# VectorE held to program order from block 2 on, with attention cut into finer steps, in a fused attention and Strassen MLP kernel

## The chip, the cores and the metric

The kernel runs on one core of a Trainium2 chip. A core has five engines that are used here: TensorE (PE, matmuls; its weight loads are shown apart as PEld), VectorE (DVE), ScalarE (ACT), GpSimd (POOL) and SyncE (SP, which here only issues transfers). They run side by side, each through a queue of its own, and wait for each other by semaphores. The metric is the time of one execution on the device, in microseconds (us), as a median of several runs. The profile is of one such execution; its span runs from the first to the last instruction and is a little shorter than the time.

## The reference, cut to what matters

```python
# q, k, v: (8, 8, 576, 64) f32, batch B, heads H, sequence S, head size D
kv  = einsum('bhsd,bhse->bhde', k, v)
out = einsum('bhsd,bhde->bhse', q, kv)
rms = sqrt(mean(out * out, axis=-1) + 1e-6)
att = out / rms * g_norm
x = att.transpose(0, 2, 1, 3).reshape(4608, 512)      # B*S tokens, H*D features
h = x @ w_in                                          # 512 -> 2048, w_in comes as float64
g = maximum(0.01 * h, h)
result = g @ w_out                                    # 2048 -> 512, w_out comes as float64
```

Attention has no softmax: a 64 x 64 matrix `kv` for each head, a product with `q`, and a division by a root mean square. Then come two dense layers with a leaky ReLU between them. The 4608 tokens are worked on in nine blocks of 512 (block 0 to block 8). A batch has 576 tokens, so a block boundary cuts through each batch: the tokens of batch b fill the end of block b and the beginning of block b + 1.

## The kernel before: the parts that matter here

Block 0 is a plain matrix product, because the weights are still arriving and being rounded to f32 (ScalarE and VectorE do that). From block 1 on both dense layers are Strassen products in Winograd's form: seven products of half-sized matrices in place of eight, with sums before and after them. From block 2 on the first layer (`h`) is cut so twice, 49 small products. The sums that belong to the weights are formed once; the sums over `x`, over `g` and over the results are formed by VectorE and GpSimd in every block, while TensorE goes on.

A block from 2 on has four parts (`c` = 0 to 3) of seven steps (`t` = 0 to 6). Call `7 * c + t` the slot, 0 to 27. In each slot TensorE does one step of `h` for this part, one step of the second layer (`o`), which runs some slots later for the part before, and in some slots a piece of attention for a later block.

```python
pin = tc.keep_in_program_order     # a pinned instruction keeps its place among the pinned of its engine;
                                   # the others are placed by the scheduler of the language's tile layer
ps_att = tile_pool(bufs=2, PSUM)   # two banks, tag "att": kv_ps and o_ps of attention share them
ps_m   = tile_pool(bufs=1, PSUM)   # six banks: ha, hb, hc, hd for h, oa, oc for o

def matmul(*args, **kw):
    pin(nc.tensor.matmul(*args, **kw))              # L112: all of TensorE's matmuls

def copy_kv(b, kv_ps):
    for i in range(2):
        nc.vector.tensor_copy(kvs[b % 2][:, i::2, :], kv_ps[i])      # L315

def add(eng, out_, a, b_, minus=False, pinned=False):
    ins = eng.tensor_tensor(out_, a, b_, ...)                        # L557: nearly all sums
    if pinned: pin(ins)

def outputs(b, lo, hi, e, sums):                    # one half (e) of q @ kv for some columns
    o_ps = [ps_att.tile([P, n], tag="att") for _ in range(2)]
    o_products(b, lo, hi, e, o_ps)                  # 8 matmuls that read kvs[b % 2] and qT
    for l in range(2):
        ...                                         # ACT square (L343); for e == 1 DVE adds it (L347)
    for l in range(2):
        nc.scalar.activation(x[:, 2 * l + e, :], o_ps[l], func=AF.Copy, scale=...)   # L349

def divide(lo, hi, sums):
    for l in range(2):
        nc.vector.transpose(t, sums[l])             # L356
        nc.vector.tensor_reduce(rms[:, l, :], ...)  # L357
    nc.scalar.activation(rms, rms, func=AF.Sqrt, ...)                # L359
    nc.vector.reciprocal(rms, rms)                  # L360
    for l in range(2):
        nc.scalar.copy(t, ...)                      # L363 "spread"
        nc.vector.transpose(inv, t)                 # L366
        nc.vector.tensor_mul(to, to, inv)           # L368

def tail_of(b, lo, hi):                             # three steps: e = 0, e = 1, divide
    ...

def attention(b, apart=True):                       # a generator; each yield ends a step
    # steps 1 to 3: turn q of pair 0 | turn q of pair 1, kv products of both | ask for loads
    # steps 4 to 7: turn q of pair 2 | turn q of pair 3 | kv products of both | copy_kv, ask for loads
    # then the tail for block b (512 - 64 b tokens), and the tail for block b + 1 (64 (b + 1) tokens)

ORDER = (1, 2, 6, 5, 7, 3, 4)                       # step t of h and of o does product ORDER[t]
# o: products 1, 6, 7, 4 go to bank oa and 2, 5, 3 to bank oc. After each product the bank is added
# to o by DVE, or, in part 0 where it is the first for its quarter of o, copied by ACT.
# So steps go oa, oc, oa, oc, oa, oc, oa, and the next part begins with oa again.

def product_h_two(i, c, quarters, to):
    into = {1: (0, True), 2: (0, False), 6: (1, True), 5: (3, True), 7: (3, False), 3: (1, False), 4: (2, True)}
    for t, k in enumerate(ORDER):
        ...                                         # 4 matmuls to ha or hc, 3 to hb or hd (128x128)
        # fresh: ACT copies both banks; else (products 2, 7, 3: t = 1, 4, 5) DVE adds both
        yield
    add(nc.vector, g21, ...); add(nc.vector, g11, ...)                   # seven sums on DVE
    add(nc.vector, g22, ...); add(nc.vector, g12, ...); add(nc.vector, g22, ...)
    add(nc.vector, g21, ...); add(nc.vector, g21, ...)
    for t in (g11, g12, g22, g21): relu(t)          # ACT, L729
    sums_of(c, to)                                  # four sums on POOL: s1, s2, s3, s4

A_SLOTS = (1, 3, 5, 8, 10, 11, 13, 14, 15, 17, 18, 19, 21)      # one step of attention in each

for i in range(1, NB):
    for c in range(NC):
        for t in range(7):
            go(h_steps, 1)
            go_o()                                  # one step of o (its step 0 falls in slots 2, 9, 16, 23)
            ...                                     # block 1: weight sums
            if 7 * c + t in A_SLOTS: go(a_steps, 1)
            load_some()
            # last part: t = 2: go(a_steps), sums over the x of the next block; t = 3, 4: inner sums on POOL
        go(h_steps)                                 # the seven g sums and what follows
```

In block 1 the first layer is a Strassen product of one level (`product_h`), which used banks `ha` and `hc` in all four parts. In block 0 attention's steps are put in by a table of half-steps: `12, 13, 15, 16, 18, 20, 22, 23, 24, 25, 26, 27`; the last three are the tail of 128 columns for block 2.

Of the kernel before, what the change touches and what calls it, by code (L numbers as in the profile page):

```python
# [23 lines left out]
def kernel(  # L24
# [63 lines left out]
    ps_m = ctx.enter_context(tc.tile_pool(name="ps_m", bufs=1, space=bass.MemoryType.PSUM))  # L88

    pin = tc.keep_in_program_order  # L90


    NW = U * NE * P
# [218 lines left out]

    def copy_kv(b, kv_ps):
        for i in range(2):
            nc.vector.tensor_copy(kvs[b % 2][:, i::2, :], kv_ps[i])  # L315

    def kv_tiles():
        return [ps_att.tile([P, NP // 2, D], F32, tag="att", name="kv_ps") for _ in range(2)]
# [1 line left out]
    def t2k(n, name):  # L320
        home = {"tag": name, "bufs": 1} if name[:3] == "sum" else {"tag": "t2k", "bufs": 3}
        return work.tile([P, n], F32, name=name, **home)

    def x_of(lo, hi):
        return block(lo // NT)[:, :, lo % NT:lo % NT + hi - lo]
# [9 lines left out]
    def outputs(b, lo, hi, e, sums):  # L335


        x, n = x_of(lo, hi), hi - lo
        o_ps = [ps_att.tile([P, n], F32, tag="att", name="o_ps") for _ in range(2)]
        o_products(b, lo, hi, e, o_ps)  # L340
        for l in range(2):
            sq = t2k(n, "sq" if e else f"sum{l}")
            nc.scalar.activation(sq, o_ps[l], func=AF.Square)  # L343
            if e == 0:
                sums.append(sq)
            else:
                nc.vector.tensor_add(sums[l], sums[l], sq)  # L347
        for l in range(2):
            nc.scalar.activation(x[:, 2 * l + e, :], o_ps[l], func=AF.Copy, scale=g_sb[:, e:e + 1])  # L349

    def divide(lo, hi, sums):
        x, n = x_of(lo, hi), hi - lo
        rms = work.tile([P, 2, n // E], F32, tag="rms", name="rms", bufs=2)
        for l in range(2):
            t = t2k(n, "turned")
            nc.vector.transpose(t, sums[l])  # L356
            nc.vector.tensor_reduce(rms[:, l, :], t.rearrange("p (a i) -> p a i", i=E),  # L357
                                    axis=AX.X, op=ALU.add)
        nc.scalar.activation(rms, rms, func=AF.Sqrt, scale=1.0 / D, bias=eps_sb)  # L359
        nc.vector.reciprocal(rms, rms)  # L360
        for l in range(2):
            t = t2k(n, "spread")
            nc.scalar.copy(t.rearrange("p (a i) -> p a i", i=E),  # L363
                           rms[:, l, :].unsqueeze(2).to_broadcast([P, n // E, E]))
            inv = t2k(n, "inv")
            nc.vector.transpose(inv, t)  # L366
            to = x[:, 2 * l:2 * l + 2, :]
            nc.vector.tensor_mul(to, to, inv.unsqueeze(1).to_broadcast([P, 2, n]))  # L368

    def tail_of(b, lo, hi):  # L370
        sums = []
        for e in range(2):
            outputs(b, lo, hi, e, sums)
            yield
        divide(lo, hi, sums)
        yield

    def attention(b, apart=True):

        qT = qTs[b] = work.tile([P, NP, S], F32, tag="qT", name="qT")  # L380
        kv_ps = kv_tiles()

        def turn(p):
            q_in = q_ins.pop((b, p))
            nc.vector.transpose(
                qT[:, p, :].rearrange("p (t s) -> p s t", s=T),
                q_in.rearrange("p (s d) -> p s d", d=D)[:, :, :32])

        for m in range(2):
            turn(2 * m)  # L390
            yield
            turn(2 * m + 1)
            if m:
                yield
            attention_kv(b, m, kv_ps)
            pairs_next = [(b + m, p) for p in ((2, 3) if m == 0 else (0, 1)) if b + m < B]
            if apart or m == 0:
                for nxt in pairs_next[:1 if apart else 2]:
                    if apart:
                        to_load.extend((*nxt, what) for what in ("q", "kv"))  # L400
                    else:
                        load_pair(*nxt)
            yield
            if apart:
                if m:
                    copy_kv(b, kv_ps)
                for nxt in pairs_next[1:]:
                    to_load.extend((*nxt, what) for what in ("q", "kv"))
                yield
        if not apart:  # L410
            copy_kv(b, kv_ps)
            yield
        for i in (b, b + 1):
            yield from tail_of(b, max(i * NT, b * S), min((i + 1) * NT, (b + 1) * S))

    def first_attention():

# [137 lines left out]

    def add(eng, out_, a, b_, minus=False, pinned=False):
        ins = eng.tensor_tensor(out_, a, b_, op=ALU.subtract if minus else ALU.add)  # L557
        if pinned:
            pin(ins)

    def sides_w1(c):
# [104 lines left out]
    def sides_x(i):  # L666
# [10 lines left out]
        sides = {1: b11, 2: b21, 3: b22, 4: t4, 5: t1, 6: t2, 7: t3}  # L677

        def sums():
            add(nc.vector, t1, b12, b11, True)  # L680
            add(nc.vector, t2, b22, t1, True)
            add(nc.vector, t3, b22, b12, True)
            add(nc.vector, t4, b21, t2, True)

        batches, quarters, at = [], {k: {} for k in ORDER}, 0
        upper, lower = (x[:, h:h + 2, :].rearrange("p r (t v n) -> p t r v n", t=2, v=2)
# [19 lines left out]
                else:  # L706
                    add(nc.gpsimd, t4, y21, t2, True)

        return sides, quarters, sums, inner

    def strassen(which, left, right, done):


        banks = {}
        for i in ORDER:
            b = "a" if i in (1, 6, 7, 4) else "c"
            if i in FRESH:
                banks[b] = ps_m.tile([P, 2, N2], F32, tag=f"{which}{b}", name=f"{which}_{b}")
            bank = banks[b]
            for part in range(2):  # L720
                for r in range(2):
                    matmul(bank[:, part, :], lhsT=left(i, part, r), rhs=right(i, part, r),
                           start=i in FRESH and part == 0 and r == 0, stop=(r == 1),
                           skip_group_check=True)
            done(i, bank.rearrange("p u (v n) -> p (u v) n", v=2))
            yield
# [20 lines left out]
    def product_h(c, w_sides, x_sides, to):  # L747

        g11, g21, g22, g12 = g_of(c)

        def done(i, bank):

            if i == 1:
                nc.scalar.copy(g11, bank)
            elif i == 5:
                nc.scalar.copy(g22, bank)
            elif i == 2:
                add(nc.vector, g11, bank, g11, pinned=True)
                relu(g11)
            elif i == 6:  # L760
                nc.scalar.copy(g21, bank)
            elif i == 3:
                add(nc.vector, g21, bank, g21, pinned=True)
                relu(g21)
            elif i == 7:
                add(nc.vector, g22, bank, g22, pinned=True)
                relu(g22)
            else:
                relu(g12, bank)

        yield from strassen("h", lambda i, part, r: w_sides[i][:, part, r, :],
                            lambda i, part, r: x_sides[i][:, r, :], done)
        sums_of(c, to)

    def product_h_two(i, c, quarters, to):
# [22 lines left out]
        g11, g21, g22, g12 = g_of(c)  # L798
        add(nc.vector, g21, qa[:, :, 0, :], qa[:, :, 1, :])
        add(nc.vector, g11, qa[:, :, 0, :], qc[:, :, 0, :])  # L800
        add(nc.vector, g22, g21, qa[:, :, 2, :])
        add(nc.vector, g12, g22, qa[:, :, 3, :])
        add(nc.vector, g22, g22, qc[:, :, 1, :])
# [6 lines left out]
    def product_o(n, g_sides, os, finish):  # L810
# [10 lines left out]
        def done(i, bank):  # L821
# [11 lines left out]
            elif i == 4:  # L833
                sums(1)

        yield from strassen("o", lambda i, part, r: g_sides[i][:, 2 * r + part, :],
                            lambda i, part, r: w_sides[i][:, r, :], done)

    def go(steps, n=None):
# [13 lines left out]
    def first_block(between):  # L853
# [26 lines left out]
        for t in range(4):  # L880
# [3 lines left out]
            else:  # L884
# [3 lines left out]
    first_attention()  # L888
    steps = {i: tail for tail in [tail_of(0, NT, S)] for i in (6, 8, 10)}
    steps.update((i, a1) for a1 in [attention(1, False)]  # L890
                 for i in (12, 13, 15, 16, 18, 20, 22, 23, 24, 25, 26, 27))
    loaded, rounded = 7, 5

    def between(n, half):
# [14 lines left out]

    first_block(between)  # L910
    x_sides, _, sums, _ = sides_x(1)
    sums()
    h_sides, more = sides_w1(0)
    more()
    for part in range(2):
# [2 lines left out]
        combine(0, part)  # L918

    A_SLOTS = (1, 3, 5, 8, 10, 11, 13, 14, 15, 17, 18, 19, 21)  # L920

    LAG = 2
    o_queue, waited = collections.deque(), 0
# [5 lines left out]
            o_queue.popleft()  # L929

    for i in range(1, NB):
        a_steps = attention(i + 1) if i + 1 < B else iter(())
        os = {}
        one = i == 1
        for c in range(NC):
            g_sides = {}
            h_steps = product_h(c, h_sides, x_sides, g_sides) if one else \
                product_h_two(i, c, quarters, g_sides)
            for t in range(7):
                go(h_steps, 1)  # L940
                if waited == LAG:
                    go_o()
                elif o_queue:
                    waited += 1
                if one:
# [6 lines left out]
                    if t == 5 and c < NC - 1:  # L952
                        more_h()
                        combine(c + 1, 1)
                if 7 * c + t in A_SLOTS:
                    go(a_steps, 1)
                load_some()
                if c == NC - 1 and i + 1 < NB:
                    if t == 2 + one:
                        go(a_steps)  # L960
                        x_sides, new_quarters, sums, inner = sides_x(i + 1)
                        sums()
                    elif t == 3 + one:
                        inner(0)
                    elif t == 4 + one:
                        inner(1)
            go(h_steps)
            if c == NC - 1 and i + 1 < NB:
# [37 lines left out]
```

## Time and profile before

| what | value |
|---|---|
| time, median of 3 runs (range) | 940.5 us (938.89 to 941.13) |
| span of the profiled execution | 937.3 us, in a run of 939.01 us |
| mean granted TensorE clock | 0.998 |
| blocks 0 and 1, up to the first two-level product | 236.5 us |
| block 2, 3, 4, 5, 6, from its first `h` product to that of the next block | 100.38, 99.30, 98.30, 98.69, 98.67 us |
| block 7 (no attention left) | 92.17 us |
| DMA, mean over the span | 213 GB/s |

The page of the profile gives busy times of the engines, the chain of work that ended last, and groups of equal instructions by line and tile. A view of the waits says which engine sat idle before which instruction, and what ended that idle time. The timeline lists single instructions or runs of equal ones: start in us, length in us, engine, line, operation, tiles, count, and in square brackets the idle time ahead of it. A matmul of f32 is recorded as two instructions, so that four matmuls of the program show as x8.

### The profile page before, as it was taken

Reading aid. Unit: us, or ns where it says so; the run is one execution under the profiler, and the core shown is the slowest. Engines: PE = TensorE matmul, PEld = TensorE weight load, DVE = VectorE, ACT = ScalarE, POOL = GpSimd, SP = SyncE. Lnnn points to the kernel's source line nnn. Section 1 sums busy time; section 2 is a strip of 40 time slices with the busy share of each in tenths; the row PEclk is TensorE's granted clock in tenths of the full one; section 3 lists DMA queues with packets and bytes.
Section 4 is the critical chain, followed back from the end, with each engine's and each line's share of the span. In section 5 each row is a group of like instructions: output and inputs, shape, how many; then the busy total and the mean of one; then the engine's idle time right before and its main releaser. Section 6 shows DMA issues by size and latency. Waiting matters only on the chain.

```text
span 937.3 us, 17990 instructions
## 1 busy us (share of the span) xinstructions
PE 921.7 (98%) x7076; PEld 774.7 (83%) x7076; DVE 597.8 (64%) x992; ACT 328.2 (35%) x659; POOL 319.1 (34%) x318
## 2 busy tenths in 40 slices
PE   8999999999999999999999999999999999999997
PEld 6544436878998899889988999899988999999996
DVE  3866894578357755596648854785578755554554
ACT  3543632242134422442234323432344233223321
POOL 2000353977622352216210722262225522532222
PEclk9999999999999999999999999999999999999999
DMA  8999925985499569956896688757856675667632
GB/s 258 189 227 244 268 100 166 292 296 164 157 321 275 163 189 274 309 160 177 255 300 205 188 238 294 225 171 236 257 171 182 195 216 183 184 196 219 188 114 90
DMA packets 90067, 200.05 MB, mean 213 GB/s; under 512 B 9856, under 2 KB 42112, under 8 KB 89984
## 3 DMA queue, kind: packets, MB, share of 16 engines
q1 hardware_dynamic: 79392, 186.85, 68.5%
q10 hardware_dynamic: 10144, 10.88, 3.5%
q8 instruction: 56, 0.92, 0.4%
q0 software_dynamic: 448, 1.18, 0.3%
q14 instruction: 27, 0.22, 0.1%
HBM read 172.39 MB, written 26.48 MB: 212 GB/s over the span
## 4 chain that ended last, share of the span: by engine, by line
PE 83%; DVE 7%; DMA 6%; ACT 2%; issue 1%; SPq 0%; ACTq 0%; DVEq 0%
PE o_a L112 22%; PE o_c L112 17%; PE h_ha L112 10%; PE h_hc L112 8%; PE h_hb L112 7%; PE h_hd L112 6%; PE h_a L112 3%; PE o_acc L112 3%; PE h_c L112 2%; PE h_ps L112 2%; DVE g L557 2%; PE o_ps L112 2%; PE kv_ps L112 2%; DMA pairs<-in_k_dram 1%; DMA q_in<-in_q_dram 1%
## 5 line engine op out<-in xcount | busy, mean ns | idle before, releaser
L557 POOL TENSOR_TENSOR gs<-g 128x512 f32<-128x512 f32 x64 | 80.4, 1277 | 446.8 <-ACT g L729 446.8
L557 DVE TENSOR_TENSOR o<-o_c,o 128x512 f32<-128x512 f32 x88 | 60.6, 689 | 98.7 <-PE o_c L112 97.0
L112 PE MATMUL o_a<-pairs,gs 128*128 128x256 f32 x512 | 121.1, 379 | 0.0
L557 DVE TENSOR_TENSOR o<-o_a,o 128x512 f32<-128x512 f32 x104 | 71.2, 685 | 78.0 <-PE o_a L112 78.0
L793 ACT COPY w_all<-h_ha 128x512 f32<-128x512 f32 x84 | 48.9, 582 | 198.6 <-PE h_ha L112 196.7
L729 ACT ACTIVATE g<-g 128x512 f32<-128x512 f32 x124 | 77.4, 630 | 102.3 <-DVE g L557 99.6
L112 PEld LDWEIGHTS o_a<-pairs,gs 128*128 128x128 f32 x512 | 93.0, 190 | 10.3
L112 PE MATMUL o_a<-w,g 128*128 128x256 f32 x256 | 61.1, 381 | 3.9 <-DVE o L557 3.6
L112 PEld LDWEIGHTS h_ha<-stage,w_all 128*128 128x128 f32 x448 | 58.0, 191 | 7.0 <-issue 2.4
L112 PE MATMUL o_c<-w,g 128*128 128x256 f32 x256 | 60.5, 379 | 0.0
L112 PE MATMUL o_c<-w,gs 128*128 128x256 f32 x256 | 60.5, 379 | 0.0
L112 PE MATMUL o_c<-pairs,gs 128*128 128x256 f32 x256 | 60.5, 379 | 0.0
L112 PE MATMUL o_a<-pairs,g 128*128 128x256 f32 x256 | 60.5, 379 | 0.0
L112 PE MATMUL h_ha<-stage,w_all 128*128 128x128 f32 x448 | 60.1, 277 | 0.0
L112 PE MATMUL h_ps<-xT,w_all 128*128 128x512 f32 (+1 forms) x136 | 58.0, 571 | 0.2 <-DVE w_all L249 0.2
L112 PE MATMUL o_acc<-w,g 128*128 128x512 f32 x128 | 58.0, 597 | 0.0
L112 PEld LDWEIGHTS o_a<-w,g 128*128 128x128 f32 x256 | 46.4, 190 | 10.1 <-DVE o L557 3.5
L557 POOL TENSOR_TENSOR pairs<-w_all 128x512 f32<-128x512 f32 x8 | 10.5, 1318 | 127.9 <-DMA stage<-in_moe_w_in_dram 97.2
L557 DVE TENSOR_TENSOR w_all<-h_hc,w_all 128x512 f32<-128x512 f32 x56 | 38.6, 689 | 22.7 <-PE h_hc L112 18.5
L557 DVE TENSOR_TENSOR g<-g,pairs 128x512 f32<-128x512 f32 x84 | 52.9, 684 | 0.0
L112 PEld LDWEIGHTS o_c<-w,gs 128*128 128x128 f32 x256 | 46.5, 190 | 5.2
L112 PEld LDWEIGHTS o_c<-pairs,gs 128*128 128x128 f32 x256 | 46.5, 190 | 5.2
(168 smaller groups left out, 1956.0 us busy)
## 6 DMA issues: line engine op xcount, KB each, us to landing
w_all<-w SPq DMA_DIRECT2D x196, 448.0 KB, 4.1
pairs<-w SPq DMA_DIRECT2D x56, 512.0 KB, 4.5
out_dram<-o ACTq DMA_DIRECT2D x36, 256.0 KB, 4.5
v_in<-in_v_dram SPq DMA_DIRECT2D x29, 288.0 KB, 5.6
k_in<-in_k_dram SPq DMA_DIRECT2D x28, 288.0 KB, 5.6
q_in<-in_q_dram SPq DMA_DIRECT2D x56, 144.0 KB, 6.5
q_in<-in_q_dram SPq DMA_DIRECT2D x56, 140.0 KB, 6.3
w<-stage SPq DMA_DIRECT2D x12, 512.0 KB, 4.6
```

The source lines that it names most:

```text
L112: pin(nc.tensor.matmul(*args, **kw))
L557: ins = eng.tensor_tensor(out_, a, b_, op=ALU.subtract if minus else ALU.add)
L729: nc.scalar.activation(t, t if src is None else src, func=AF.Prelu, alpha=SLOPE)
L793: nc.scalar.copy(q[:, at], banks[tag])
```

## The change

From block 2 on every VectorE instruction is pinned, so that VectorE does its work in the order in which the program is written, and no longer in the order that the scheduler picks. So that the written order is a good one, attention is cut finer (the division into five steps in place of one), its steps get slots of their own, and they are put between the slot's `h` step and its `o` step. The last two of a batch's steps fall into slots 3 and 4 of the next block. The sums over `x` are spread over slots 22 to 24. The first two of the seven `g` sums are made ahead of the `o` step of slot 6 of a part, the other five after it. In block 1, `h` takes banks `ha`, `hc` and `hb`, `hd` by turns. In block 0 the last three steps of attention move from half-steps 25, 26, 27 to 26, 28, 29. The arithmetic is the same.

The purpose is that a sum which TensorE is waiting for (an `o` bank that has to be added before it can be written again) doesn't stand behind a long piece of attention in VectorE's queue.

```diff
+    def in_turn(ins):
+        if steady:
+            pin(ins)
...  # copy_kv, the transposes, reductions, reciprocals and products of attention: in_turn(...)
     def divide(lo, hi, sums):
...
+            if l:
+                nc.scalar.activation(rms, rms, func=AF.Sqrt, scale=1.0 / D, bias=eps_sb)
+            yield                                   # step: transpose and reduce, one l each
+        in_turn(nc.vector.reciprocal(rms, rms))
...      # ACT: both spreads
+        yield
+        for l in range(2):
+            in_turn(nc.vector.transpose(inv, spread[l]))
+            in_turn(nc.vector.tensor_mul(to, to, ...))
+            yield
...  # attention(b, fine=True): the two tails, seven steps each, are taken in this order
+        for tail in (0, 0, 0, 0, 0, 1, 0, 0, 1, 1, 1, 1, 1, 1):
+            next(tails[tail])
+            yield
...
     def add(eng, out_, a, b_, minus=False, pinned=False):
-        if pinned:
+        if pinned or steady and eng is nc.vector:
             pin(ins)
...  # product_h
-        yield from strassen("h", ...)
+        yield from strassen((("ha", "hc"), ("hb", "hd"))[c % 2], ...)
...  # product_h_two
         add(nc.vector, g11, qa[:, :, 0, :], qc[:, :, 0, :])
+        yield
         add(nc.vector, g22, g21, qa[:, :, 2, :])
...
-                 for i in (12, 13, 15, 16, 18, 20, 22, 23, 24, 25, 26, 27))
+                 for i in (12, 13, 15, 16, 18, 20, 22, 23, 24, 26, 28, 29))
...
+    FINE_SLOTS = {1: 1, 2: 1, 4: 1, 9: 1, 10: 2, 11: 2, 12: 1, 15: 1, 16: 1, 17: 2, 18: 1, 19: 2,
+                  22: 1, 24: 1, 25: 1}
+    LATE_SLOTS = (3, 4)
...
+        one = i == 1
+        steady = not one
+        late, a_steps = a_steps, attention(i + 1, fine=not one) if i + 1 < B else iter(())
...
             for t in range(7):
+                slot = 7 * c + t
                 go(h_steps, 1)
+                if not one:
+                    if t == 6:
+                        go(h_steps, 1)              # two of the g sums
+                    if slot in LATE_SLOTS:
+                        go(late, 1)
+                    for _ in range(FINE_SLOTS.get(slot, 0)):
+                        go(a_steps, 1)
+                    if i + 1 < NB:
+                        if slot == 22:
+                            x_sides, new_quarters, sums, inner = sides_x(i + 1)
+                        if slot in (22, 23, 24):
+                            go(sums, 2 if slot == 23 else 1)
+                        if slot == 24:
+                            inner(0)
+                        elif slot == 25:
+                            inner(1)
+                    load_some()
                 ...                                 # then the o step, as before
```

## The prediction

> **What bounds the kernel now.** I read the page's busy times and its chain first.
>
> ```profile
> PE 921.7 (98%) x7076; PEld 774.7 (83%) x7076; DVE 597.8 (64%) x992; ACT 328.2 (35%) x659; POOL 319.1 (34%) x318
> PE 83%; DVE 7%; DMA 6%; ACT 2%; issue 1%; SPq 0%; ACTq 0%; DVEq 0%
> ```
>
> TensorE is busy for 98% of the span and carries 83% of the chain. Since no matmul is removed, the change can only win the time in which TensorE stands still. The waits of TensorE by what ended them (line, who was waited for, total us, times, longest):
>
> ```profile
> PE o_a L112 <- DVE o L557: 3.6, 3, 1.8
> PE o_ps L112 <- ACT xT L349: 1.3, 1, 1.3
> PE h_a L112 <- ACT g L729: 0.7, 1, 0.7
> ```
>
> These three are what the change aims at. The other waits fall in the first 31 us or after the last matmul. To see where the 3.6 us are I read the timeline around the end of block 2 (start, length):
>
> ```profile
> 319.23 0.83 PE L112 MATMUL h_hb<-stage,w_all 128*128 128x128 f32 x6
> 319.74 1.14 DVE L368 TENSOR_TENSOR xT<-xT,inv 128x512 f32<-128x512 f32 x1
> 320.80 0.43 DVE L366 STREAM_TRANSPOSE inv<-spread 128x256 f32<-128x256 f32 x1
> 321.16 0.65 DVE L557 TENSOR_TENSOR o<-o_a,o 128x512 f32<-128x512 f32 x1
> 321.86 1.99 PE L112 MATMUL o_a<-w,g 128*128 128x256 f32 x8 [1.80 <-DVE o L557]
> ```
>
> This is slot 23. Bank oa's last product must be added before the next part's first product may overwrite it, and the add stands behind attention's division. The same place costs 0.73 us at 421.17 in block 3. In blocks 4 to 6 I compared the start of the o_a matmul with that of the h_hb matmul ahead of it: 0.67 us in quiet slots, but 618.15 - 617.21 = 0.94 in block 5 and 716.83 - 715.89 = 0.94 in block 6. The third wait of 1.11 us is at 920.83, in the last part of the last block.
>
> A quiet slot gives the unit for everything below (block 8, slot 25):
>
> ```profile
> 906.24 0.38 PE L112 MATMUL h_ha<-xT,w_all 128*128 128x128 f32 x2
> 907.40 0.69 DVE L557 TENSOR_TENSOR w_all<-h_ha,w_all 128x512 f32<-128x512 f32 x1 [0.27 <-PE h_ha L112]
> 907.80 1.89 PE L112 MATMUL o_a<-pairs,gs 128*128 128x256 f32 x8
> 908.07 0.56 DVE L557 TENSOR_TENSOR pairs<-h_hb,pairs 128x384 f32<-128x384 f32 x1
> 106.43 0.46 DVE L315 COPY kv<-kv_ps 128x128 f32<-128x128 f32 x2
> ```
>
> (The last line, from block 0, is the pair of copies that the reckoning of slot 11 needs.) With T the slot's start: h takes TensorE until T+1.56, o until T+3.29, where the next slot begins. VectorE adds the first h bank from T+1.16 to T+1.85 and the second to T+2.39; the add of an o bank can start 1.93 after its matmuls began (907.80 to 909.73).
>
> **What the Trainium skill says.** "PSUM — Partial Sum Buffer", section "Engine vs sequencer instructions", says that VectorE's queue is strictly first in, first out and that matmuls start and complete in program order. The trace agrees: at 321.86 TensorE stands for an add that waits for nothing but its turn. So the order of the two queues decides, and one can read it off the built programs without any time. "SBUF — State Buffer", section "Who interferes with whom", says that a VectorE instruction with two SBUF inputs and a GpSimd instruction that reads SBUF exclude each other, and the second waits for the first to end. The trace agrees: GpSimd's sum of g at 619.71 began 0.07 us behind a VectorE product of 1.07 us and took 2.14 us, where its like take 1.28. "Perfetto Trace Analysis", section "Identifying the Most-Contended Engine", warns that busy matmul time overstates; weight loads are the better measure. In the stretch from 335.2 to 434.4 us (most of block 3) they are 88.83 of 99.2 us, and since the distances between o products are 3.29 us throughout, I take TensorE as really full.
>
> **The change part by part.**
>
> Block 0: the wait of 1.29 us at 126.40 is attention's second o_ps product of 128 columns, one half-step after the first, when ScalarE has not yet emptied the banks. Now it comes two half-steps later, each about 3.5 us of matmuls. All of it should go: -1.3.
>
> Block 1: the wait of 0.69 us at 162.18 is the second part's first product, for bank ha that ScalarE is still reading. With two pairs of banks it goes: -0.7.
>
> Blocks 2 to 6, slot 23: 1.80 + 0.73 + 0.27 + 0.27 + 0.05 (block 7, start of o_a at 739.96) = 3.1 us. In the new order only small pieces stand ahead of that add. -3.1, less what comes back in slot 22 below.
>
> New wait, slot 11. FINE_SLOTS gives slot 11 two steps: step 7, which is copy_kv, and step 8, attention's first o_ps products. Those matmuls read kvs and take the two banks that kv_ps held, so they need the copies twice over. In the built order TensorE's queue has for slot 11: h_ha, h_hb, o_ps, o_a. VectorE's has: add of h_ha, add of h_hb, two copies, and both copies are now pinned behind the adds. By the quiet slot, which is the same step of h (product 7): adds end at T+2.39, the second copy starts about 0.06 before that and two take 0.46 (the pair at 106.43), so they end at T+2.79; with 0.1 for the semaphore (the add at 321.16 ended at 321.81 and TensorE began at 321.86; at 920.83 it was 0.15) o_ps starts at T+2.89. It could have started at T+1.65 (0.09 after h, as o_ps at 303.69 after o_a). That is 1.24 us in which TensorE stands, and nothing later gives it back, because TensorE is full. Five blocks have it (batches 3 to 7, in blocks 2 to 6): 5 x 1.24 = +6.2. Before, the copies ran some ten us ahead of the products: the first at 278.8, the o_ps at 288.7.
>
> Slot 22. New ahead of the critical add: transpose and reduce of one l (for 256 to 512 columns 0.41 + 0.40 up to 0.69 + 0.68), and one x sum (0.65). I count from S, the start of slot 20 in which the part ends, with offsets from the last part of block 8 (S = 912.82) and 0.6 from one queued VectorE sum to the next. The first g sum starts at S+1.8 (914.59), the second ends by S+3.0; the oa add starts at S+3.5 (914.38 + 1.93); five g sums end at S+7.1; the oc add of slot 21 ends at S+7.7; the h adds of slot 22 (which starts at S+6.58) end at S+8.9. Then come 0.7 to 1.3 of transpose and reduce, then 0.6, so the add starts at S+10.2 to S+10.8 and frees the bank at S+11.0 to S+11.6. TensorE wants it at S+11.43 (two slots and h of 1.56 further on, from S+3.29 each). That is nearly free. But GpSimd makes its four sums of the part at about S+8 to S+13, and the x sum has two SBUF inputs, so it may wait up to one of those sums (1.28). With half of that, the five blocks lose about 0.1, 0.3, 0.4, 0.6 and 0.7 = 2.1; without it 0.1. I take +1.2.
>
> Slot 1 of each block: one q transpose (1.24) ends at S+10.15, before the add is ready at S+10.07 + 0.04, so it costs nothing.
>
> The tail. At the end of block 8 the add of o22 from oa now stands after two g sums and not after three. It can't start before 916.40, while VectorE is free at 915.8. The five remaining sums, then two o adds follow, all 0.6 later; the last bank is free at 921.3 and not at 920.7: +0.6.
>
> Sum: -1.3 - 0.7 - 3.1 + 6.2 + 1.2 + 0.6 = +2.9, so 940.5 + 2.9 = 943.4 us.
>
> **Rivals.**
>
> First: slot 11 costs nothing, for instance since the adds of h come earlier than in my quiet slot or the copies slip ahead. Then it is 943.4 - 6.2 = 937.2 us. For it speaks that the slots look as if they had been chosen with care; against it the two orders, which leave no room.
>
> Second: in strict order VectorE meets many small waits, which the scheduler had filled with other work. VectorE is at 64%, so no single queue is too long, but a q transpose that waits for its transfer (6.5 us from issue to landing, and 4.6 us of such waits before) would hold every add behind it. Against it: the q loads are asked for seven slots, some 23 us, ahead of the slot that turns them. If each of five blocks lost another 2 us, it would be 953.
>
> Third: GpSimd's lock bites in slot 22 in full, or also in slots 3 and 4 (products of 1.1 to 1.8 us). That adds 2 to 3 us: 946.
>
> **Range and chances.** The gains are bounded by the trace at 5.1 us, so the time can't fall under 935.4, which is 0.5% less. The losses rest on one wait, counted five times, that I hold for nine parts in ten sure, with 0.3 us either way, and on two smaller ones. Runs of the kernel before differ by 2.2 us. So 938.5 to 947 us 8 times in 10. Faster by over 2% (under 921.7) is ruled out by the waits there are: 0.01, kept for what I don't see. Slower by over 2% (above 959.3) needs the second rival at twice its size: 0.02. Within 2%: 0.97.
>
> **What would show it.** In TensorE's waits the three lines above shrink: o_ps on ACT xT and h_a on ACT g are gone, o_a on DVE o keeps about 1.7 us at the tail and up to 1 us in each slot 23. A new line stands on top: o_ps waiting for DVE kv (copy_kv), five times about 1.2 us. Blocks 2 to 6, from one first h product to the next, take 99.6 to 100.3 us each in place of 98.3 to 100.4, block 4 (98.3, without a wait now) showing the loss most plainly. I am wrong if that line is missing, or if TensorE waits at other places for more than 2 us in all.

## The result, and the profile after

| | before | after |
|---|---|---|
| time, median (range) | 940.8 us (938.89 to 942.32, 4 runs) | 945.8 us (943.97 to 947.01, 4 runs) |
| ratio after / before | | 1.0052, 95% interval 1.0027 to 1.0078 |
| span of the profiled execution | 937.3 us | 944.6 us |
| start to the first `h` product of block 0 | 28.60 us | 30.20 us |
| block 0, from there to the first `h` product of block 1 | 119.24 us | 118.54 us |
| block 1 | 88.64 us | 87.89 us |
| blocks 2 to 6 | 100.38, 99.30, 98.30, 98.69, 98.67 us | 100.31, 100.31, 100.32, 100.31, 100.32 us |
| block 7 | 92.17 us | 92.12 us |
| block 8 and the end | 113.31 us | 114.28 us |

The kernel became 0.5% slower. The spans differ by 7.3 us. 1.6 of that lies ahead of all work that was changed: the first products wait for the input's transfers, and over all profiles of this study, of whatever kernel, that point lies between 28.5 and 30.4 us. Where the change acts, the profiles differ by -0.70 (block 0), -0.75 (block 1), +6.2 (blocks 2 to 6) and +0.97 (the end): +5.7 us.

The page of the kernel after shows the busy times and the chain that ended last:

```profile
PE 923.4 (98%) x7076; PEld 780.9 (83%) x7076; DVE 611.1 (65%) x992; ACT 327.9 (35%) x659; POOL 320.9 (34%) x318
PE 88%; DVE 6%; DMA 3%; issue 1%; POOL 1%; ACT 1%; DVEq 0%; ACTq 0%; POOLq 0%
```

The busy shares say nothing of the loss: all are as before. Of the chain TensorE has 88% in place of 83%, and yet the time is longer. The waits of TensorE (who, for whom, total us, times, longest) do say it:

```profile
PE o_ps L118 <- DVE kv L321: 5.5, 6, 1.0
PE o_a L118 <- DVE o L582: 4.5, 6, 2.1
PE o_acc L118 <- ACT g L896: 0.7, 1, 0.7
```

The two waits for ScalarE that the change aimed at are gone (`o_ps` on `xT`, `h_a` on `g`), but all three lines here hold losses of the new order. The first has five new waits of 1.0 in slot 11 of blocks 2 to 6 (the sixth, 0.5, was there before, in the first attention). The second was 3.6 in three waits, long ones in blocks 2 and 3, and is 4.5 in six: a wait in slot 23 of each block and one of 2.1 at the end, where it was 1.1. The third is new.

The timeline of slot 11 of block 2 after the change:

```profile
276.78 0.69 DVE L582 TENSOR_TENSOR w_all<-h_ha,w_all 128x512 f32<-128x512 f32 x1 [0.20 <-PE h_ha L118]
277.45 0.56 DVE L582 TENSOR_TENSOR pairs<-h_hb,pairs 128x384 f32<-128x384 f32 x1
277.93 0.48 DVE L321 COPY kv<-kv_ps 128x128 f32<-128x128 f32 x2
278.36 0.97 PE L118 MATMUL o_ps<-qT,kv 64*32 64x320 f32 x16 [1.01 <-DVE kv L321]
```

The copies of `kv` stand behind both adds of `h`, and TensorE stands until they are done: taken singly, one product starts at 278.36, 0.15 after the end of the first copy (278.21), and the others from 278.56 on, 0.15 after the end of the second (278.41). This slot takes 5.25 us in block 4; with the copies made earlier it takes 3.97 (below).

The end of part 2 of the same block, slots 22 and 23:

```profile
318.24 2.50 POOL L582 TENSOR_TENSOR gs<-g 128x512 f32<-128x512 f32 x2 [19.51 <-ACT g L753]
319.08 0.43 DVE L363 STREAM_TRANSPOSE turned<-sum 128x256 f32<-128x256 f32 x1
319.55 0.42 DVE L364 TENSOR_REDUCE rms<-turned 128x8 f32<-128x256 f32 x1
319.89 1.40 DVE L582 TENSOR_TENSOR w_all<-xT 128x512 f32<-128x512 f32 x1
321.21 0.68 DVE L582 TENSOR_TENSOR o<-o_a,o 128x512 f32<-128x512 f32 x1
321.94 1.99 PE L118 MATMUL o_a<-w,g 128*128 128x256 f32 x8 [0.48 <-DVE o L582]
```

The sum over `x` takes 1.40 us, and ends 0.55 after GpSimd's pair of sums (318.24 + 2.50 = 320.74). The add that TensorE waits for stands behind it. In block 6 the transpose and the reduction are twice as large, so that the `x` sum comes later in the queue, and still it ends 0.55 after GpSimd's pair:

```profile
719.51 2.50 POOL L582 TENSOR_TENSOR gs<-g 128x512 f32<-128x512 f32 x2 [20.39 <-ACT g L753]
721.69 0.87 DVE L582 TENSOR_TENSOR w_all<-xT 128x512 f32<-128x512 f32 x1
722.48 0.68 DVE L582 TENSOR_TENSOR o<-o_a,o 128x512 f32<-128x512 f32 x1
```

That is why slot 23 takes 4.03 to 4.04 us in all five blocks, 0.75 more than the 3.29 of a quiet slot, whatever the length of the pieces ahead. The waits of before, uneven (100.38 in block 2, 98.30 in block 4), became the same loss of 1.28 + 0.75 in each.

The last part of block 8, first before and then after:

```profile
916.40 0.68 DVE L557 TENSOR_TENSOR o<-o_a,o 128x512 f32<-128x512 f32 x1
917.00 0.68 DVE L557 TENSOR_TENSOR g<-g,w_all 128x512 f32<-128x512 f32 x1
917.60 1.89 DVE L557 TENSOR_TENSOR g<-g,pairs 128x512 f32<-128x512 f32 x3
920.83 1.96 PE L112 MATMUL o_a<-w,g 128*128 128x256 f32 x8 [1.11 <-DVE o L557]
```

```profile
922.64 0.69 DVE L582 TENSOR_TENSOR o<-o_a,o 128x512 f32<-128x512 f32 x1 [0.43 <-PE o_a L118]
923.25 1.48 DVE L582 TENSOR_TENSOR g<-g,w_all 128x512 f32<-128x512 f32 x2
924.76 2.02 DVE L582 TENSOR_TENSOR g<-g,pairs 128x512 f32<-128x512 f32 x3
926.70 0.69 DVE L582 TENSOR_TENSOR o<-o_c,o 128x512 f32<-128x512 f32 x1
928.13 1.96 PE L118 MATMUL o_a<-w,g 128*128 128x256 f32 x8 [2.07 <-DVE o L582]
```

Two things add up to the 0.96 more. VectorE stands for 0.43 ahead of the `oa` add, where before it made a third `g` sum. And the five sums after it take 926.70 - 923.25 = 3.45 us, 0.69 each, where the four before took 2.40 (917.00 to 919.40), 0.60 each. In the written order, which is pinned now, three of them read or overwrite what the sum just ahead of them touched; the scheduler had set such pairs apart. Taken singly, these three start 0.72 to 0.79 after the sum ahead of them, and the other two, like the `oc` add, about 0.61 after it.

### The profile page after: what moved, and what is told of

It reads as the page before. It is cut to its first block, busy times and chain, and to the rows that moved or that the text cites. A ratio compares the mean times of both kernels' runs of the same rounds, so it can differ in the third digit from the quotient of the medians.

```text
span 944.6 us, 17997 instructions
## 1 busy us (share of the span) xinstructions
PE 923.4 (98%) x7076; PEld 780.9 (83%) x7076; DVE 611.1 (65%) x992; ACT 327.9 (35%) x659; POOL 320.9 (34%) x318
## 4 chain that ended last, share of the span: by engine, by line
PE 88%; DVE 6%; DMA 3%; issue 1%; POOL 1%; ACT 1%; DVEq 0%; ACTq 0%; POOLq 0%
PE o_a L118 22%; PE o_c L118 18%; PE h_ha L118 10%; PE h_hc L118 8%; PE h_hb L118 7%; PE h_hd L118 6%; PE o_acc L118 4%; PE h_ps L118 4%; PE o_ps L118 2%; PE kv_ps L118 2%; PE h_a L118 1%; PE h_c L118 1%; DMA pairs<-in_v_dram 1%; PE h_b L118 1%; DVE w_all L582 1%
## 5 line engine op out<-in xcount | busy, mean ns | idle before, releaser
L582 DVE TENSOR_TENSOR g<-g,pairs 128x512 f32<-128x512 f32 x84 | 55.6, 689 | 1.9
L118 PEld LDWEIGHTS o_c<-w,g 128*128 128x128 f32 x256 | 46.4, 190 | 8.6 <-issue 3.1
```

## The experiments

The theory after the comparison: the loss of blocks 2 to 6 is two places, both of them pieces that program order now holds in front of (or behind) an add that frees a bank. The copies of `kv` cost 1.28 a block; the first `x` sum costs 0.75, by GpSimd's exclusion more than by its length. The rival: strict order costs many small waits, and moving a piece only shifts them.

**The copies of `kv` left to the scheduler.** Only the two copies are not pinned; in the built order they then come right behind the q transpose of slot 10.

```diff
-            in_turn(nc.vector.tensor_copy(kvs[b % 2][:, i::2, :], kv_ps[i]))
+            nc.vector.tensor_copy(kvs[b % 2][:, i::2, :], kv_ps[i])
```

> The changed kernel with one thing undone: the two copies of kv are not pinned. The built VectorE queue then has them right behind the q transpose of slot 10, ahead of the o add and of slot 11's h adds; TensorE's queue and the loads stay. Theory (the copies stand behind the h adds of slot 11): the five waits of o_ps on DVE kv go, each slot 11 shrinks from 5.25 us (block 4) to 3.97 as slot 12, so -1.28 x 5 = -6.4 us against the changed kernel, about 939.4 us, 0.998 to 1.000 of the kernel before. Rival (the two steps in one slot are too close whatever the queue's order, since o_ps needs the banks of kv_ps): the waits stay and the time stays at about 945.8.

Measured: 940.7 us, ratio to before 1.0006 (0.9995 to 1.0017). In block 2 the copies are done long before the products that need them:

```profile
274.72 0.49 DVE L321 COPY kv<-kv_ps 128x128 f32<-128x128 f32 x2 [3.14 <-PE kv_ps L118]
278.08 0.77 PE L118 MATMUL o_ps<-qT,kv 64*32 64x320 f32 x16
```

Slot 11 takes 4.18, 4.08, 3.97, 3.86 and 3.76 us in blocks 2 to 6 (attention's products get smaller), where it took 5.46, 5.36, 5.25, 5.13 and 5.04: 1.28 in each. Blocks 2 to 6 take 99.03 to 99.05. Slot 23 stays at 4.03 to 4.05. So by the profiles the pinned copies are worth 6.4 us, more than the whole loss. The medians are 5.1 apart (945.8 and 940.7), within their scatter.

**The first `x` sum one slot later.**

```diff
-                        if slot == 22:
+                        if slot == 23:
                             x_sides, new_quarters, sums, inner = sides_x(i + 1)
-                        if slot in (22, 23, 24):
-                            go(sums, 2 if slot == 23 else 1)
+                        if slot in (23, 24):
+                            go(sums, 3 if slot == 23 else 1)
```

> The changed kernel with the first sum over x moved from slot 22 to slot 23, so that only the transpose and the reduce of attention stand ahead of the add that frees bank oa. Theory (the x sum holds the add up): the five waits of o_a on DVE o in slot 23 go (0.75 us each with the refill), -3.75 us against the changed kernel: about 942.0 us, ratio 1.001. Rival (transpose and reduce are what is too long): the waits shrink by half at most in the blocks with few columns (256) and stay in those with many (448, 512): about 944.5 us.

Measured: 943.25 us, ratio to before 1.0030 (1.0021 to 1.0038). Slot 23 takes 3.28 to 3.29 in all blocks, blocks 2 to 6 take 99.56 to 99.58, and slot 11 is as in the changed kernel. Slots 22 and 23 of block 2 in this kernel's timeline:

```profile
318.43 2.50 POOL L582 TENSOR_TENSOR gs<-g 128x512 f32<-128x512 f32 x2 [19.53 <-ACT g L753]
320.13 0.69 DVE L582 TENSOR_TENSOR o<-o_a,o 128x512 f32<-128x512 f32 x1
320.73 0.74 DVE L582 TENSOR_TENSOR w_all<-xT 128x512 f32<-128x512 f32 x1
321.51 1.64 DVE L582 TENSOR_TENSOR w_all<-xT,w_all 128x512 f32<-128x512 f32 x1
```

The add of the bank now runs beside GpSimd's sums: one of its inputs is in PSUM, and it takes its usual 0.69. The `x` sums still wait for GpSimd (1.64 for one), but nothing waits for them there.

**Length or exclusion?** In the place of that first `x` sum stands a transpose of the same 128x512, which reads one SBUF tile and takes as long (0.70). The sum itself is left out, so one operand of the next block's products is not what it should be; the work of TensorE is the same.

```diff
-                add(nc.vector, t, a, b, True)
+                if t is t1 and steady:
+                    pin(nc.vector.transpose(t1.rearrange("p r n -> p (r n)"), x[:, 0, :]))
+                else:
+                    add(nc.vector, t, a, b, True)
```

> The changed kernel with the first x sum of slot 22 replaced by a transpose of the same 128x512 elements (0.69 us by its like, against 0.65 for the sum): the sum b12 - b11 is left out, what is in its place has one SBUF input and not two. The queue is as long as before. Theory (lock: the sum waits for GpSimd's running sum to end): the piece takes 0.69 us in place of 1.40 and the waits of o_a on DVE o in slot 23 fall from 0.48 to 0 in the blocks with 256 to 384 columns and to at most 0.2 in the last two. Rival (length of the queue alone): the waits stay at 0.48 or grow.

Measured in one run: 944.7 us, a time that is not to be compared: in this run's last part the granted clock was 0.94 (from 915 to 942 us), and eight matmuls took 3.65 us there in place of 1.96. The slots are what counts. In block 2 the transpose keeps its length beside GpSimd's pair, and the add follows it at once:

```profile
317.27 2.50 POOL L582 TENSOR_TENSOR gs<-g 128x512 f32<-128x512 f32 x2 [19.53 <-ACT g L756]
318.91 0.70 DVE L707 STREAM_TRANSPOSE w_all<-xT 128x512 f32<-128x512 f32 x1
319.54 0.65 DVE L582 TENSOR_TENSOR o<-o_a,o 128x512 f32<-128x512 f32 x1
```

Slot 23 takes 3.31, 3.45, 3.58, 3.71 and 3.85, that is 0.02 to 0.56 over a quiet slot, 1.45 in all, and it grows with the size of the pieces ahead. With the two-input sum it was 0.75 in every block, 3.75 in all. So of the loss in slot 23, 1.45 is queue length and 2.3 is the exclusion. The length alone cost more than I had expected.

**A third `g` sum ahead of slot 6's `o` step.** Everything else as in the changed kernel.

```diff
-        yield
         add(nc.vector, g22, g21, qa[:, :, 2, :])
+        yield
```

> The changed kernel with three and not two g sums ahead of slot 6's o step. Theory (at the tail VectorE stands still for 0.4 us before the oa add, and g22 and g12, of which the second reads what the first wrote, stand back to back and lose another 0.3): the wait of o_a at the tail falls from 2.07 to about 1.1 us as in the kernel before, and the sums g22 and g12 no longer stand together for 1.48 us. Rival (only the lost 0.6 counts): it falls to about 1.4. In the steady blocks nothing changes: the waits of slots 11 and 23 stay at 1.0 and 0.5 us.

Measured in one run: 943.1 us. The wait at the end is 1.4 and not 1.1, as the rival said: the 0.43 of idle time is gone, but of the three dependent sums two still stand right behind the sum that they depend on, and start 0.72 after it. What I had not expected is slot 23: 3.33 to 3.38 in blocks 2 to 5, 4.57 in block 6. The timeline of blocks 2 and 6 shows why:

```profile
319.20 1.04 DVE L582 TENSOR_TENSOR w_all<-xT 128x512 f32<-128x512 f32 x1
319.66 1.72 POOL L582 TENSOR_TENSOR gs<-gs,g 128x512 f32<-128x512 f32 x1
...
718.19 1.27 POOL L582 TENSOR_TENSOR gs<-gs,g 128x512 f32<-128x512 f32 x1
718.27 1.75 DVE L582 TENSOR_TENSOR w_all<-xT 128x512 f32<-128x512 f32 x1
720.67 2.00 PE L118 MATMUL o_a<-w,g 128*128 128x256 f32 x8 [1.02 <-DVE o L582]
```

GpSimd's pair now ends earlier, 0.3 after slot 23 begins and not 1.0: it waits for ScalarE's relus of the `g` sums, and the third of these sums comes sooner. So the 0.75 of slot 23 depends on the order of the `g` sums as well as on the exclusion. In block 2 the `x` sum stood ready before GpSimd's third sum began, ran first, and GpSimd waited (1.72 in place of 1.27). In block 6, behind larger pieces, it came 0.08 us after GpSimd had begun, and took 1.75. The same two instructions, and the one that is 0.08 late pays a microsecond. The section "Who interferes with whom" of the Trainium skill's "SBUF — State Buffer" says that the order of issue decides who blocks; the numbers here agree.

**The two small parts of the change alone.** The kernel before with `h` of block 1 in two pairs of banks and the moved half-steps of block 0.

```diff
-        yield from strassen("h", ...)
+        yield from strassen((("ha", "hc"), ("hb", "hd"))[c % 2], ...)
...
-                 for i in (12, 13, 15, 16, 18, 20, 22, 23, 24, 25, 26, 27))
+                 for i in (12, 13, 15, 16, 18, 20, 22, 23, 24, 26, 28, 29))
```

> The kernel before with only the two small parts of the change: block 1's h in two pairs of banks, and the last three half-steps of block 0 moved; VectorE from block 2 on as before. Theory: block 0 gains 0.55 to 0.7 us and not 1.29, since the wait for the banks goes but a wait of 0.74 for ScalarE comes (o_acc on ACT g); block 1 gains 0.7. So 1.3 us less than the kernel before, ratio 0.9986, and the three waits of o_a for DVE o (3.6 us in all) stay. Rival: the 0.74 comes from the division in five steps elsewhere and is missing here; then block 0 gains 1.29 and the ratio is 0.9979.

Measured: 940.1 us, ratio 0.9995 (0.9987 to 1.0002). Block 1 takes 88.05, 0.59 less than before. Block 0 takes 119.08, 0.16 less: `o_ps` no longer waits, but the new wait is 1.29 and not 0.74. The waits of this kernel:

```profile
PE o_a L112 <- DVE o L557: 3.6, 3, 1.8
PE o_acc L112 <- ACT g L871: 1.3, 1, 1.3
```

So the theory had the place right and the size wrong: it depends on what else the scheduler has put ahead of the division on VectorE. The rival, that the wait comes from the finer steps, falls.

**Slots and finer steps, but VectorE not pinned.**

```diff
-        steady = not one
+        steady = False
```

> The changed kernel with all its slots and fine steps, but VectorE's instructions from block 2 on not pinned: the scheduler places them. Theory: slot 11 has no wait (the copies come ahead of the o add), which is worth 6.4 us; the x sums are placed ahead of o adds in some blocks, which costs up to 1 us in slots 22 and 23 of each; blocks 2 to 6 take 98.3 to 99.5, the ratio to the kernel before is 0.997 to 1.001. Rival: the fine steps and slots alone remove the waits for the o banks, program order is not needed; then blocks 2 to 6 take 98.3 each and the ratio is 0.9945.

Measured: 940.1 us, ratio 0.9991 (0.9982 to 1.0001). Slot 11 has no wait. Slot 23 takes 3.42, 5.07, 3.66, 3.45 and 3.29, and blocks 2 to 6 take 98.94, 100.07, 98.66, 98.45 and 98.29 (block 2 loses 0.52 more in slot 6). The long one, in block 3:

```profile
414.78 1.25 DVE L402 STREAM_TRANSPOSE qT<-q_in 128x576 f32<-128x576 f32 x1
416.29 1.26 POOL L582 TENSOR_TENSOR gs<-gs,g 128x512 f32<-128x512 f32 x1
416.38 1.85 DVE L381 TENSOR_TENSOR xT<-xT,inv 128x640 f32<-128x640 f32 x1
418.16 0.68 DVE L582 TENSOR_TENSOR o<-o_a,o 128x512 f32<-128x512 f32 x1
418.89 2.00 PE L118 MATMUL o_a<-w,g 128*128 128x256 f32 x8 [1.51 <-DVE o L582]
```

It is not the `x` sums, as I had thought, but a q transpose and one of attention's products, which is caught behind GpSimd (1.85, where the next of its kind takes 0.83). That is the old fault of slot 23 over again. So finer pieces in these slots do not remove it while the scheduler places them. Whether the moves of the next version would do so without pinning was not tried. The profiled execution is the fastest of this kernel's 20 runs (936.4 us), and its blocks 2 to 6 are only 3.0 us longer than those of the next kernel, while the medians lie 5.1 apart; its profile also has an earlier start (28.48 and 29.66 us) and a shorter block 1 (87.86 and 88.15), and what the other runs lose beyond that is not known.

**All three losses undone, in program order.** The copies one slot earlier, the `x` sums from slot 23 on, three `g` sums ahead of slot 6's `o` step, and the others in an order in which dependent sums stand apart.

```diff
-    FINE_SLOTS = {..., 10: 2, 11: 2, ...}
+    FINE_SLOTS = {..., 10: 3, 11: 1, ...}
...  # x sums: 3 in slot 23, 1 in slot 24, as above
     # g sums, written by what they form; "|" is the o step of slot 6
-    # g21, g11 | g22, g12, g22, g21, g21
+    # g21, g11, g22 | g21, g12, g21, g22
```

> The changed kernel with all three losses undone at once, VectorE still in program order: copies of kv one slot earlier (slot 10), x sums from slots 22 to 24 to slots 23 and 24, three g sums ahead of slot 6's o step and the sums that depend on each other set apart. Theory: the gains add up, 6.4 + 3.75 + 0.9 = 11 us less than the changed kernel; blocks 2 to 6 take 98.30 each, the tail's wait is 1.1 as before the change, the only waits left are that and the 0.74 in block 0. Ratio to the kernel before 0.9945 (about 935.5 us). Rival: a move only shifts the wait (the copies to slot 10's o add, the x sums to slot 24's); then blocks 2 to 6 take 99 or more and the ratio is 0.998 or more.

Measured: 934.9 us (5 runs), ratio to before 0.9942 (0.9929 to 0.9954). Blocks 2 to 6 take 98.28 to 98.30 each, 10.1 us less than in the changed kernel; block 8 and the end take 113.30, 0.98 less. The waits:

```profile
PE o_a L118 <- DVE o L582: 1.1, 1, 1.1
PE o_acc L118 <- ACT g L896: 0.7, 1, 0.7
PE o_ps L118 <- DVE kv L321: 0.5, 1, 0.5
```

The medians differ by 945.8 - 934.9 = 10.9 us, 11 were expected; by the two ratios to the kernel before it is 10.3. The moves do not shift the waits elsewhere; the rival falls. This version is faster than both kernels.

**The same with block 0's last half-steps 25, 27, 28.**

```diff
-                 for i in (..., 24, 26, 28, 29))
+                 for i in (..., 24, 25, 27, 28))
```

> As the run before it, and in block 0 the last half-steps are 25, 27, 28 in place of 26, 28, 29. Theory: the wait of o_acc for ScalarE (0.74) came from the division standing ahead of the last relu of block 0, so one half-step earlier it is gone, and the wait for the o_ps banks (1.29 before) does not come back, since two half-steps still lie between the two products: 0.7 us less than the run before it, ratio to the kernel before 0.9938. Rival: the wait for the banks comes back in part, or the relu still stands behind the division; then no difference.

Measured: 936.2 us, ratio 0.9956 (0.9942 to 0.9970). The wait of `o_acc` grew to 2.04, and block 0 takes 119.83 in place of 118.53. The theory fell: ScalarE's queue isn't in program order, and here the scheduler put the division's root ahead of the last two relus and not of one:

```profile
141.05 0.30 ACT L367 ACTIVATE rms<-rms,eps_sb 128x8 f32<-128x8 f32 x1 [5.49 <-DVE rms L364]
141.76 0.50 ACT L373 COPY spread<-rms 128x128 f32<-128x128 f32 x2 [0.41 <-DVE rms L369]
142.16 1.08 ACT L896 ACTIVATE g<-h_ps 128x512 f32<-128x512 f32 x2
142.80 7.13 PE L118 MATMUL o_acc<-w,g 128*128 128x512 f32 x16 [2.04 <-ACT g L896]
```

ScalarE stands idle for 5.49 us for VectorE's reductions, with two relus behind the root. The first of them could have run in that time, since its `h_ps` products ended at 133.9; those of the second ended at 140.8, just ahead of the root. (This run also lost 1.2 us in block 2, where a load of weights came late; I have not followed that up.)

**Relus first.** As the version with the moves, but the last half-step is 30, and ScalarE's last two relus of block 0 and the root are pinned among each other.

```diff
-                nc.scalar.activation(rms, rms, func=AF.Sqrt, ...)
+                root = nc.scalar.activation(rms, rms, func=AF.Sqrt, ...)
+                if not steady and hi - lo == 128:
+                    pin(root)
...
-                nc.scalar.activation(gT, h_ps, func=AF.Prelu, ...)
+                relu = nc.scalar.activation(gT, h_ps, func=AF.Prelu, ...)
+                if n >= 14:
+                    pin(relu)
...
-                 for i in (..., 26, 28, 29))
+                 for i in (..., 26, 28, 30))
```

> As the version with the moves, but the third of block 0's last half-steps is 30 in place of 29, and ScalarE's last two relus of block 0 and that division's root are pinned, so that in ScalarE's queue the root stands behind the last relu. Theory: the wait of o_acc for ACT g (0.74 with the moves, 1.29 with the banks and half-steps alone, 2.04 with the earlier half-steps) is only this order: the root waits for VectorE's reductions and holds the relu behind it. The wait is then gone, block 0 takes 117.8 in place of 118.53, o_ps does not wait, and the time is 0.7 less, ratio to the kernel before 0.9934. Rival: the relu itself comes late, as TensorE's h product ends just ahead of it; then a wait of 0.5 or more stays and the ratio is 0.994.

Measured: 934.5 us (6 runs), ratio to before 0.9930 (0.9912 to 0.9949). The intervals of this version and the one with the moves overlap, so the times alone don't tell them apart; the profile does. No wait of `o_acc` is left, block 0 takes 117.52 in place of 118.53, and the order is seen on ScalarE:

```profile
141.08 7.03 PE L118 MATMUL o_acc<-w,g 128*128 128x512 f32 x16
141.28 0.60 ACT L898 ACTIVATE g<-h_ps 128x512 f32<-128x512 f32 x1 [5.53 <-PE h_ps L118]
143.80 0.30 ACT L367 ACTIVATE rms<-rms,eps_sb 128x8 f32<-128x8 f32 x1 [1.92 <-DVE rms L364]
```

The root still waits for VectorE, behind the relu now, and TensorE runs through. The later half-step and the pins were changed together; which of them was needed is not shown.

## Why the prediction was right, point by point

The time fell into the predicted range and within 2%: 945.8 against 943.4. The medians show 5.0 us of loss (2.5 to 7.3 by the interval), the profiles 5.7 without the start; 2.9 were predicted. Its terms, against the profiles:

| step of the prediction | predicted | measured |
|---|---|---|
| block 0, wait of `o_ps` | -1.3 | -0.70 |
| block 1, wait of `h_a` | -0.7 | -0.75 |
| slot 23, old waits | -3.1 | -3.84 |
| slot 11, copies of `kv` | 5 x 1.24 = +6.2 | 5 x 1.28 = +6.4 |
| slot 22, transpose, reduction and `x` sum | +1.2 | +3.75 |
| end of block 8 | +0.6 | +0.97 |
| sum | +2.9 | +5.8 |

**Slot 11 was right**, in place, cause and size: read off the two queues of the built program and a quiet slot, 1.24 against 1.28. The products behind the second copy start 2.93 after the slot's begin where 2.89 was predicted, and with the copies made earlier they start at 1.65, as predicted. The first rival (the slot costs nothing) was wrong. Leaving out this one effect brings the time back to that of before (1.0006).

**Slot 22 is the term that was mis-sized**, by 2.55 us of an error of 2.9. That the other errors (+0.60 in block 0, -0.74 in the old waits, +0.37 at the end, +0.2 in slot 11) nearly cancel is luck. Two steps of it failed. First, "five g sums end at S+7.1" took 0.6 for each sum. In the written order they take 0.69 each, 0.45 more in all, and from there on everything in that queue is 0.45 later. Added to the reckoning, the five blocks lose between 0.0 and 0.6, which is what the one-input run shows (0.02 to 0.56). Second, "with half of that" for the exclusion: the `x` sum ends 0.55 after GpSimd's pair in every block, early or late in the queue, so the loss is one and the same and not growing. The third rival, GpSimd's lock in slot 22 in full (946 us), was closest to what happened, although slots 3 and 4 of which it spoke cost nothing: block 7 and the quiet slots are unchanged.

**Block 0** lost half of its gain because I looked only at who frees the banks. The moved division brings its root to the end of block 0, where the scheduler of ScalarE puts it ahead of the last relu. The wait is 0.74 here, 1.29 with the half-steps alone, 2.04 one half-step earlier, and none with the relus first. "All of it should go" holds for that wait; a new one took its place.

**Block 1**: the wait for bank `ha` is gone, but the -0.75 is one draw. In this profile TensorE waits there 0.2 us for a load of `v`, in that of the run with free copies 1.0, and in the kernel before not at all. Over the ten profiles that have the new block 1 it takes 87.86 to 88.62 us, so 0.02 to 0.78 less than before.

**The end**: the idle 0.43 and the 0.45 of dependent sums, where I had counted one sum of 0.6.

**The old waits** were worth 3.84 and not 3.1, because I added up idle times. A wait shown as 1.80 made its slot 2.07 longer (5.36 against 3.29), one of 0.73 made it 1.00 longer; and the new ones, shown as 1.01 and 0.48, cost 1.28 and 0.75. In each case 0.27 is missing from the idle time. For the waits of `o_a` the parts are these: in a quiet slot the `o` product begins 0.67 after `h_hb`, ahead of the modelled end of a run of 0.83 (0.16), and after a wait the eight matmuls take 1.99 in place of 1.89 (0.10), together 0.26. In slot 11 they are others: the one product that starts ahead ends the idle time 0.20 before the rest can start, and the first 0.07 lies under the modelled end of `h_hb`. That both come to 0.27 is chance.

The second rival, many small waits of strict order, did not happen: with three moves, program order gives five blocks of 98.28 to 98.30. In the reckoning of slot 1 the transpose ends 0.04 after the add is ready (S+10.15 against S+10.11) and not before it; it still cost nothing, as slot 1 takes 3.29 in block 4.

## What to carry to other kernels

When an engine is put in program order, everything in its queue becomes a deadline for what stands behind it: go slot by slot through what the busiest engine needs next, and let only what it needs soonest stand in front. Pinning came out ahead here only with the right order (0.9942); with the wrong one it lost 0.5%. How much of the 0.9942 the moves would give without pinning is not shown. Measure a wait by how much longer its slot became, not by the idle time shown.

A piece that another engine can hold up, like the `x` sum here (0.65 us alone, 0.87 to 1.40 behind GpSimd's pair), is best put where nobody waits for it, for its length is not its own. And what is moved takes all its parts along: the division moved for the sake of a bank brought a ScalarE root in front of a relu.

## What I had not expected of the hardware

A VectorE sum of two SBUF tiles and a GpSimd sum shared almost no time: the `x` sum, 0.65 us alone, ended 0.55 after GpSimd's pair in all five blocks, whenever it began, while an add with one input in PSUM kept its 0.69 beside the pair. Coming 0.08 us too late made the same sum take 1.75 and not 1.04 us, and TensorE's slot lose 1.28 and not 0.04 to 0.09.

VectorE sums of 128x512 f32 follow each other every 0.60 us though each is recorded with 0.68, if they don't depend on each other; five sums of which several touch what the one before them touched took 0.69 each. The Trainium skill's "VectorE: DVE Perf Modes", section "The DRAIN you can't avoid", says that the next operation does not start until the pipeline is empty, and that one which is not held starts earlier; here independent sums overlap by 0.08 in the records, so that the order of a chain of sums is worth some tenths of a microsecond. Of the 0.45 that the five sums lost, nearly all lies at the three that touch what the one before them touched, for only these start late (0.72 to 0.79 after it). With them set apart every sum starts 0.60 after the one before, though that run also had one sum more ahead of the `o` add.
